# Order and queues of the first loads in a two-layer attention and gated-MLP kernel

## The chip, the cores and the metric

The kernel runs on one core of one Trainium2 chip. The metric is device time in microseconds (us). Before the change it was 1616.12 us, the median of three executions (1615.79 to 1616.38). The whole argument is about the first 23 us of those 1616. "Fast" is the state of an execution with an undisturbed clock.

An execution has a *span*, from its first instruction to its last. The profile shows it, and it is about 1.8 us shorter than the device time.

## The reference, cut to what matters

The input is `x` of 2048 tokens by 1024 features in bf16. Two layers follow, each an attention block (sliding window of 8 keys, stride 2) and a gated MLP, with a layernorm in front of each block. The opening does only this:

```python
xn  = layernorm(x)              # 2048 x 1024
q   = xn @ wqkv[:, 0:1024]      # the query third comes first
```

For the first 512 tokens (one chunk) the kernel computes `q` from four *tiles* of 128 tokens (`x_sb[0]` to `x_sb[3]`, 256 KB each) and eight *rows* of the weight (128 x 1024, 256 KB each). Row k is what the features 128k to 128k+127 are multiplied by. These are 3 MB of first loads.

## The kernel before

The kernel builds a list of operations with estimated durations. `place()` simulates them and fixes each engine's order. Each engine executes in that order, and waits are by semaphore.

```python
def dma(kb, dst, src, reads, writes, cls=3, transpose=False, queue="SP"):
    def emit(op):
        if queue == "AQ":
            nc.scalar.dma_start(dst, src)       # ScalarE's queue
        elif transpose:
            nc.sync.dma_start_transpose(dst, src)
        else:
            nc.sync.dma_start(dst, src)         # SyncE's queue
    return pr.add(queue, 0.45, emit, reads, writes, cls, size=kb * 1024)

def q_first():
    for hh in range(2):                          # tile 0 in two halves, one on each queue
        dma(128, x_sb[0][:, hh * 512:(hh + 1) * 512], ..., queue="AQ" if hh else "SP")
    dma(256, x_sb[1][:], xin[:, 1, :], ..., queue="AQ")       # tile 1
    rows = q_weights(0, "k", load=False)
    for kk in range(4):
        rows[2](kk)                              # weight rows 0 to 3, SyncE
    load_x(0, 2, 4)                              # tiles 2 and 3, SyncE
    rows[2](4)
    rows[2](5)
    # VectorE sums half of tile 0, ScalarE the other half ...
    rows[2](6, 2, queue="AQ", after=[("part", 1)])   # rows 6 and 7 as one load, ScalarE
    # mean of tile 1 on ScalarE; tiles 0 and 1 are centred, transposed on TensorE, copied out ...
    # ... [cut] ...
    # partial products of tiles 0 and 1: rows 0-2 for tile 0, then for tile 1, then rows 3-7 for both
    for kk, j0, j1 in [(k, j, j + 1) for j in range(2) for k in range(3)] + [(k, 0, 2) for k in range(3, KT)]:
        ...  # 8 matmuls of 128x128 or 128x256, waiting for row kk
    # then "the second query half": tiles 2 and 3 against all eight rows, 64 matmuls of 128x256
```

TensorE's order in the opening is fixed: tile 0's transposes; rows 0 and 1 for tile 0 (16 matmuls); tile 1's transposes; row 2 for tile 0, rows 0 to 2 for tile 1, then row by row for both; transposes of tiles 2 and 3 in front of row 7; row 7; the second half.

The loads draw on eight DMA semaphores. The first eight loads are issued at once, each later one waits at issue until the load that last used its semaphore has landed.

## Time and profile before

| what | us | view |
|---|---|---|
| span of the profiled execution | 1614.2 | page |
| PE (TensorE matmul) busy | 1601.5, 99% | page |
| PE idle before the matmuls of row 4 | 0.91 | timeline |
| row 4 issued, landed | 5.71, 11.11 | chain of waits, single DMA records |

The page's busy time of the engines, and its chain of work that ended last, by engine and by line:

```profile
PE 1601.5 (99%) x7463; PEld 762.6 (47%) x7610; DVE 1121.5 (69%) x1904; ACT 331.3 (21%) x527; POOL 5.2 (0%) x28
...
PE 99%; DMA 1%; issue 0%; SPq 0%; DVE 0%
PE bank L347 98%; DMA slot<-in_A_wqkv_dram 1%; PE bank L523 0%; PE bank L509 0%; PE bank L428 0%; SPq L261 0%; DVE x L688 0%
```

TensorE is the limit, and the only other share that shows at all is 1% of the chain spent waiting for weights. One caution: 7463 matmuls are recorded against 7610 weight loads. 147 matmul records are missing, and each leaves a hole that looks like idle time.

TensorE's timeline in the opening of the kernel before (start and duration in us, line, operation, count; in brackets the idle time in front and what ended it):

```profile
4.98 0.66 PE L428 MATMUL bank<-ident,xn 128*128 128x128 bf16 x8
5.89 1.05 PE L509 MATMUL bank<-hT,slot 128*128 128x128 bf16 x16 [0.25 <-DVE hT L433]
6.96 0.62 PE L428 MATMUL bank<-ident,xn 128*128 128x128 bf16 x8
7.42 2.83 PE L509 MATMUL bank<-hT,slot 128*128 128x128 bf16 x40
11.16 2.79 PE L509 MATMUL bank<-hT,slot 128*128 128x256 bf16 x24 [0.91 <-DMA slot<-in_A_wqkv_dram]
13.79 1.06 PE L428 MATMUL bank<-ident,xn 128*128 128x128 bf16 x16
14.68 1.04 PE L509 MATMUL bank<-hT,slot 128*128 128x256 bf16 x8
15.56 7.15 PE L523 MATMUL bank<-xnT,slot 128*128 128x256 bf16 x64
```

L428 are transposes, L509 the partial products, L523 the second query half, which ends at 15.56 + 7.15 = 22.71. The 0.91 us at 11.16 is the wait for row 4. How it came about is in the chain in order of time, same kernel (start, duration, what):

```profile
1.66 4.03 DMA slot<-in_A_wqkv_dram
5.70 0.02 issue
5.71 5.40 DMA slot<-in_A_wqkv_dram
```

Row 1 was issued at 1.66 and landed 4.03 later. That freed its semaphore, so SyncE could issue row 4 at 5.71, and row 4 took 5.40 us, because tiles 2 and 3 and rows 6-7 were in front of it. The DMA queues of the kernel before, from 5 to 7 us (q1 is SyncE's, q10 ScalarE's; packets, MB, share of the 16 engines' time):

```profile
q1 hardware_dynamic: 403, 0.74, 101.3%
q10 hardware_dynamic: 2, 0.00, 0.5%
```

The same view of the same kernel from 7 to 9 us:

```profile
q10 hardware_dynamic: 266, 0.51, 67.1%
q1 hardware_dynamic: 148, 0.27, 36.1%
```

Rows 6-7, issued on ScalarE at 3.57, moved almost nothing from 5 to 7 us (0.5%) and had two thirds of the engines after that.

### The profile page before, as it was taken

What the parts mean: (1) busy time and instruction counts of PE and PEld (TensorE: products, weight loads), DVE (VectorE), ACT (ScalarE), POOL (GpSimd) and SP (SyncE); (2) the same over time, 40 slices, a digit from 0 to 9 for tenths busy, and PEclk for the clock granted to TensorE, in tenths of its full rate; (3) what the DMA queues carried; (4) which work ended last, traced back from release to release, by engine and by line L of the source; (5) the groups of instructions that cost most, each with busy time, mean ns of one, the idle gap of its engine ahead of it and who ended that gap; (6) DMA issues with size and microseconds to landing.
All of it is one profiled execution on the core that took longest, in us unless ns stands there. A gap on an engine that the chain in (4) does not pass through costs nothing.

```text
span 1614.2 us, 19079 instructions
## 1 busy us (share of the span) xinstructions
PE 1601.5 (99%) x7463; PEld 762.6 (47%) x7610; DVE 1121.5 (69%) x1904; ACT 331.3 (21%) x527; POOL 5.2 (0%) x28
## 2 busy tenths in 40 slices
PE   9999999999999999999999999999999999999999
PEld 6555544444444444444444444444444444444444
DVE  5898888889889888888898729884288832211211
ACT  5423322021211222113211032110321101101110
POOL 1000000000000000000000000000000000000000
PEclk9999999999999999999999999999999999999999
DMA  9834755395548664758645487365873464454451
GB/s 320 228 100 150 224 170 171 118 225 168 171 136 251 195 190 132 217 167 234 189 136 160 160 243 231 122 173 176 253 221 119 158 181 156 144 176 150 156 165 44
DMA packets 350777, 285.80 MB, mean 177 GB/s; under 512 B 72288, under 2 KB 344928, under 8 KB 350688
## 3 DMA queue, kind: packets, MB, share of 16 engines
q1 hardware_dynamic: 350128, 283.67, 58.2%
q8 instruction: 59, 0.97, 0.2%
q10 hardware_dynamic: 560, 0.92, 0.2%
q14 instruction: 30, 0.25, 0.0%
HBM read 238.94 MB, written 29.36 MB: 166 GB/s over the span
## 4 chain that ended last, share of the span: by engine, by line
PE 99%; DMA 1%; issue 0%; SPq 0%; DVE 0%
PE bank L347 98%; DMA slot<-in_A_wqkv_dram 1%; PE bank L523 0%; PE bank L509 0%; PE bank L428 0%; SPq L261 0%; DVE x L688 0%
## 5 line engine op out<-in xcount | busy, mean ns | idle before, releaser
L347 PE MATMUL bank<-xnT,slot 128*128 128x512 bf16 x4955 | 1088.9, 379 | 5.3
L347 PEld LDWEIGHTS <-slot 128*128 128x128 bf16 x5056 | 518.1, 102 | 573.0
L347 PE MATMUL bank<-slot,hT 128*128 128x512 bf16 (+2 forms) x1812 | 387.3, 372 | 1.9
L658 DVE TENSOR_TENSOR hT<-sg,bank 128x512 bf16<-128x512 bf16 x224 | 153.4, 685 | 213.0 <-PE bank L347 196.3
L265 DVE TENSOR_TENSOR scr<-scr 128x1024 bf16<-128x1024 bf16 (+3 forms) x576 | 292.1, 535 | 2.1
L347 PEld LDWEIGHTS <-hT 128*128 128x128 bf16 x1848 | 178.5, 98 | 208.7
L656 ACT ACTIVATE sg<-bank 128x512 bf16<-128x512 f32 x224 | 133.8, 597 | 653.8 <-PE bank L347 613.6
L265 DVE TENSOR_TENSOR scr<-qT,kT 128x2048 bf16<-128x2048 bf16 x128 | 153.7, 1216 | 71.7 <-DMA kT<-qkv_d 70.1
L405 ACT CAST sgt<-bank 128x512 bf16<-128x512 f32 x184 | 107.9, 586 | 290.9 <-PE bank L347 273.1
L265 DVE TENSOR_TENSOR scr<-pA,vT 128x2048 bf16<-128x2048 bf16 x128 | 152.5, 1216 | 0.4
L688 DVE TENSOR_TENSOR x<-x,bank 128x512 bf16<-128x512 bf16 (+1 forms) x66 | 43.7, 669 | 122.7 <-PE bank L347 122.4
L347 PE MATMUL bank<-wo,oT 128*128 128x512 bf16 x502 | 112.6, 379 | 0.5
L313 DVE BATCH_NORM_STATS2 st<-x 128x6 f32<-128x512 bf16 x124 | 81.5, 679 | 11.5 <-DMA x<-in_A_x_dram 11.0
L347 PEld LDWEIGHTS <-oT 128*128 128x128 bf16 x512 | 50.1, 98 | 60.3
L633 DVE TENSOR_TENSOR x<-x,bank 128x512 bf16<-128x512 bf16 x64 | 43.9, 685 | 36.5 <-PE bank L347 35.0
L320 ACT ACTIVATE sd<-mv,epst 128x4 f32<-128x4 f32 (+1 forms) x17 | 5.1, 299 | 182.4 <-DVE mv L316 181.9
L616 DVE STREAM_TRANSPOSE pA<-pB 128x2048 bf16<-128x2048 bf16 x16 | 37.0, 2310 | 0.4
L593 DVE STREAM_TRANSPOSE pB<-pA 128x2048 bf16<-128x2048 bf16 x16 | 37.0, 2310 | 0.4
L656 ACT ACT_TABLE_LOAD x20 | 25.7, 1283 | 51.3 <-PE bank L347 51.1
L265 DVE TENSOR_TENSOR pA<-scr 128x256 bf16<-128x256 bf16 x128 | 35.3, 282 | 0.3
L327 DVE TENSOR_SCALAR xn<-x,mv,rstd 128x1024 bf16<-128x1024 bf16 x62 | 30.8, 541 | 4.6 <-DMA xnT<-xn 4.5
L265 DVE TENSOR_TENSOR oT<-scr 128x256 bf16<-128x256 bf16 x128 | 33.6, 282 | 0.1
(60 smaller groups left out, 210.0 us busy)
## 6 DMA issues: line engine op xcount, KB each, us to landing
slot<-in_B_w_dram SPq DMA_DIRECT2D x160, 1024.0 KB, 5.8
slot<-in_A_wqkv_dram SPq DMA_DIRECT2D x28, 1024.0 KB, 5.2
qkv_d<-sgt SPq DMA_DIRECT2D x92, 256.0 KB, 3.4
qT<-qkv_d SPq DMA_DIRECT2D x16, 512.0 KB, 5.0
slot<-in_B_w_dram SPq DMA_DIRECT2D x16, 512.0 KB, 5.5
kT<-qkv_d SPq DMA_DIRECT2D x14, 544.0 KB, 6.6
vT<-qkv_d SPq DMA_DIRECT2D x14, 544.0 KB, 5.7
out_dram<-x SPq DMA_DIRECT2D x31, 128.0 KB, 4.2
```

Source lines behind the costliest of these rows:

```text
L265: return lambda _: nc.vector.tensor_tensor(o, a, b, op=op)
L313: dve(0.67, lambda _, hh=hh: nc.vector.bn_stats(st[q][:, j, hh, :], x_sb[n][:, hh * 512:(hh + 1) * 512]), [("x", n, hh)] + list(after), [( ...
L320: act(0.3, lambda _: nc.scalar.activation(sd[q][:, j0:j1], mv[q][:, j0:j1, 1], ACTF.Sqrt, bias=epst[:]), [("mv", q, j) for j in range(j0, ...
L327: dve(0.5, lambda _: nc.vector.tensor_scalar(xn[j][:], x_sb[n][:], mv[q][:, j, 0:1], rstd[q][:, j:j + 1], op0=ALU.subtract, op1=ALU.mult), ...
L347: nc.tensor.matmul(bank[a.bank][:, 0:ncol], lhsT=w, rhs=r, start=first and i == 0, stop=last and i == n - 1)
L405: evac(act, 0.59, lambda _, a=a, i=i, m=m: nc.scalar.copy(sgt[i][:, m % 2, :], bank[a.bank][:]), op, [], [("sgt", i, m % 2)], a)
L593: dve(2.31, lambda _: nc.vector.transpose(psmT[:].rearrange("p c d -> p (c d)"), psm[:].rearrange("p w s -> p (w s)")), allA, ["pB"])
L616: dve(2.31, lambda _: nc.vector.transpose(At[:].rearrange("p w s -> p (w s)"), AeT[:].rearrange("p c d -> p (c d)")), ["pB"], allA)
L633: evac(dve, t1(512), lambda _, xs=xs, a=a: nc.vector.tensor_tensor(xs, xs, bank[a.bank][:], op=ALU.add), op, [("x", n, hh)], [("x", n, hh) ...
L656: evac(act, 0.6, lambda _, i=i, a=ag: nc.scalar.activation(sg[i][:], bank[a.bank][:], ACTF.Silu), og, [], [("sg", i)], ag, table="silu")
L658: evac(dve, t1(512), lambda _, i=i, a=au, f=f: nc.vector.tensor_tensor(hT[:, f, :], sg[i][:], bank[a.bank][:], op=ALU.mult), ou, [("sg", i ...
L688: evac(dve, t1(cn), lambda _, xs=xs, a=a, cn=cn: nc.vector.tensor_tensor(xs, xs, bank[a.bank][:, 0:cn], op=ALU.add), op, [("x", n, hh)], [ ...
```

## The change

Its intent: the first loads come in the order in which TensorE needs them, on two queues. ScalarE's holds three at once (half of tile 0, tile 1, row 2), then tile 2. SyncE's has the rest.

```diff
         dma(256, x_sb[1][:], xin[:, 1, :], [], [("x", 1, 0), ("x", 1, 1)], 0, queue="AQ")
         rows = q_weights(0, "k", load=False)
         wslots[0] = rows[:2]
-        for kk in range(4):
+        for kk in (0, 1, 3, 4):
             rows[2](kk)
-        load_x(0, 2, 4)
-        rows[2](4)
+        rows[2](2, queue="AQ")
+        load_x(0, 3, 4)
         rows[2](5)
+        rows[2](6, 2)
... [cut]
-        rows[2](6, 2, queue="AQ", after=[("part", 1)])
+        dma(256, x_sb[2][:], xin[:, 2, :], [("part", 1)], [("x", 2, 0), ("x", 2, 1)], 0, queue="AQ")
... [cut]
         for j in range(2, TPC):
-            stats(j)
+            stats(j, [("ce", 1, 0)])
```

In the compiled instruction streams TensorE, VectorE and GpSimd keep exactly the same order. ScalarE swaps two tiny square roots, and the loads move.

## The prediction

> **What bounds the kernel now.** TensorE: the page gives PE busy 1601.5 of 1614.2 us, and the chain of waits is 99% PE, 98% of it the big matmul line. In the timeline only three PE idle times exceed 0.06 us, all in the opening: 0.15 before the first transposes (4.98), 0.25 before the first projection matmul (5.89), 0.91 (10.25 to 11.16) before the partial products of weight rows 4 and later. The rest are 0.05 us pieces, one per 49 matmuls, and a fixed tail. So the change can win little over 0.91.
>
> **Why the 0.91 is there.** Row 4 landed at 11.11. It was issued only at 5.71: eight DMA semaphores are used in turn, so the ninth and later loads wait, at issue, for the load eight before (tile 3 for row 0, landed 4.96; row 4 for row 1, landed 5.70). Tile 2 (issued 3.08), rows 6-7 (ScalarE, 3.57) and tile 3 went ahead, though needed later. From 5 to 15 us the DMA moves 383 to 392 GB/s (256 KB each 0.67 us): order is the limit. The Trainium skill, "DMA: Bandwidth & Descriptors", section "Issuing engines are not separate DMA queues", says that loads of both issuers share 16 engines and interleave; the trace agrees on the shared rate. Yet rows 6-7, issued at 3.57, got almost no packets from 5 to 7 us (0.5% of engine time against 101%) and 67% in 7 to 9: service roughly follows issue order.
>
> **What the change does.** No instruction added or removed; PE, DVE and POOL orders are identical, ScalarE swaps two tiny roots. The first eight loads (no wait) become halves of tile 0, rows 0, 1, 3, 4, tile 1, row 2. Then tile 3 waits for tile 0's first half (3.3), tile 2 on ScalarE for row 0 (about 5.0), row 5 for row 1, rows 6-7 after it. Estimates from 0.67 us per 256 KB: rows 1 and 2 share and land near 6.4 (row 1 was 5.70, row 2 6.53), row 3 at 7.2, row 4 at 7.9, tile 3 at 8.6, tile 2 at about 9, row 5 at 9.9, rows 6-7 at 11.2. PE wants row 4 at 10.25, row 5 at 11.2, row 6 at 12.1: the 0.91 goes. Transposes of tiles 2 and 3 would be wanted at 13.1; they should be ready at 12.7 and 13.3, just in time.
>
> **Cost.** ScalarE now issues tile 2 at 5.0 to 5.4 (one issue takes 0.39 us), in front of its mean of tile 1, which started at 5.24. That mean, and so tile 1's transposes (6.96), moves by about 0.2 us. PE has 0.02 us of slack there, so some 0.2 comes back as a new wait at 7 us.
>
> **Sum.** -0.91 + 0.2 = -0.7 us, all on the critical path. Predicted 1615.4 us, range 1614.8 to 1616.1. Chances: faster by over 2% 0.005, within 0.99, slower 0.005.
>
> **What would show it.** Timeline: no PE idle near 10.3; row 4 landing near 8; second query half ending 0.7 us earlier (22.7 before); mean of tile 1 at 5.4 to 5.5; PE idle of 0.1 to 0.3 near 7.
>
> **What would make it wrong.** Tiles 2 and 3 land after 9.5 and the wait moves to the transposes near 13 us (gain 0.3 or less); row 1 lands past 6.6; ScalarE's issue costs nothing (gain 0.9); K weights or DMA transposes, wanted at 22.0, come late; chips differ by more than the effect.

## The result, and the profile after

The median is 1615.36 us (six executions, 1615.13 to 1616.30) against 1616.09 for the kernel before (six, 1615.79 to 1616.38), so 0.73 us less. The ratio is 0.9997, with an interval of 0.9984 to 1.001. (A ratio is the mean time of one kernel's fast runs over that of the other's of the same rounds, so not quite the ratio of the medians quoted.) The mean gained less than the median, because one of the six took 1616.30. The profile fell on just that one.

TensorE's timeline in the opening of the changed kernel, that execution:

```profile
5.02 1.00 PE L428 MATMUL bank<-ident,xn 128*128 128x128 bf16 x8
6.15 0.61 PE L510 MATMUL bank<-hT,slot 128*128 128x128 bf16 x8
7.03 0.62 PE L510 MATMUL bank<-hT,slot 128*128 128x128 bf16 x8 [0.27 <-DMA slot<-in_A_wqkv_dram]
7.57 0.62 PE L428 MATMUL bank<-ident,xn 128*128 128x128 bf16 x8
8.03 4.58 PE L510 MATMUL bank<-hT,slot 128*128 128x128 bf16 x56
13.40 1.05 PE L510 MATMUL bank<-hT,slot 128*128 128x256 bf16 x8 [0.79 <-DMA slot<-in_A_wqkv_dram]
14.28 1.06 PE L428 MATMUL bank<-ident,xn 128*128 128x128 bf16 x16
15.18 1.04 PE L510 MATMUL bank<-hT,slot 128*128 128x256 bf16 x8
16.05 7.15 PE L524 MATMUL bank<-xnT,slot 128*128 128x256 bf16 x64
```

(Lines have moved by one: L510 and L524 are L509 and L523 of before.) The wait for row 4 is gone: 56 matmuls run through from 8.03. Two waits are new, 0.27 us in front of row 1's matmuls and 0.79 us in front of row 6's. The second half ends at 23.20, later than the 22.71 of before. The chain in order of time, changed kernel:

```profile
1.66 5.32 DMA slot<-in_A_wqkv_dram
6.98 0.02 issue
7.00 0.33 SPq L261
7.32 0.04 issue
7.37 5.98 DMA slot<-in_A_wqkv_dram
```

Row 1, issued at 1.66 as before, took 5.32 us instead of 4.03. Rows 6-7, issued at 7.37, took 5.98 us and landed at 13.35. The DMA queues of the changed kernel, from 5 to 7 us:

```profile
q1 hardware_dynamic: 287, 0.52, 71.1%
q10 hardware_dynamic: 138, 0.25, 33.7%
```

Row 2, issued on ScalarE at 1.69 (0.03 us after row 1 on SyncE), does take a third of the engines while row 1 is wanted. From 5 to 6 us alone it is half: 50.5% for ScalarE's queue, 52.3% for SyncE's. Sums from 9 to 12 us in the changed kernel (busy of PE, PEld, DVE, ACT, POOL, then clock, DMA share, GB/s):

```profile
9.00:12.00 3.00, 3.00 (x38) 2.77 (x36) 2.31 (x5) 2.31 (x6) 0.00 (x0) 1.00 0.88 288
```

Before, this stretch had a DMA share of 1.05 and 395 GB/s. Fewer bytes moved here, while rows 5 to 7 were on their way.

The times at which the loads landed, each read from its single DMA record in the traces (us; the last four columns are experiments):

| load | before | after | after_again | after_third | order_one_queue | tile2_act_only |
|---|---|---|---|---|---|---|
| row 0 | 4.96 | 5.38 | 5.01 | 4.81 | 4.94 | 4.90 |
| tile 1 | 5.15 | 5.57 | 5.21 | 5.01 | 5.18 | 5.19 |
| row 1 | 5.70 | 6.98 | 7.03 | 7.40 | 5.83 | 5.85 |
| row 2 | 6.53 | 7.30 | 7.23 | 8.15 | 6.81 | 6.68 |
| row 4 | 11.11 | 8.34 | 8.39 | 9.01 | 8.39 | 8.51 |
| tile 2 | 8.65 | 9.66 | 9.72 | 10.35 | 9.07 | 8.74 |
| tile 3 | 10.44 | 9.01 | 9.16 | 9.74 | 9.76 | 9.41 |
| row 5 | 11.79 | 10.65 | 10.34 | 10.99 | 10.39 | 10.06 |
| rows 6-7 | 9.74 | 13.35 | 12.21 | 12.36 | 11.75 | 11.43 |

### The profile page after: what moved, and what is told of

It is laid out like the page before. It is cut to its first block, busy times and chain, and to the rows that moved or that the text cites. A ratio compares the mean times of both kernels' runs of the same rounds, so it can differ in the third digit from the quotient of the medians.

```text
span 1614.5 us, 19227 instructions
## 1 busy us (share of the span) xinstructions
PE 1609.9 (100%) x7610; PEld 763.0 (47%) x7610; DVE 1121.6 (69%) x1904; ACT 330.8 (20%) x527; POOL 5.3 (0%) x28
## 4 chain that ended last, share of the span: by engine, by line
PE 99%; DMA 1%; SPq 0%; issue 0%; DVE 0%
PE bank L347 98%; DMA slot<-in_A_wqkv_dram 1%; PE bank L524 0%; PE bank L510 0%; SPq L261 0%; PE bank L428 0%; DVE x L689 0%
## 5 line engine op out<-in xcount | busy, mean ns | idle before, releaser
L313 DVE BATCH_NORM_STATS2 st<-x 128x6 f32<-128x512 bf16 x124 | 81.5, 680 | 12.2 <-DMA x<-in_A_x_dram 11.8
```

The source lines that it names most:

```text
L313: dve(0.67, lambda _, hh=hh: nc.vector.bn_stats(st[q][:, j, hh, :], x_sb[n][:, hh * 512:(hh + 1) * 512]), [("x", n, hh)] + list(after), [( ...
```

## The experiments

**How they were built.** A first attempt only edited the load lines. In the build, `place()` then settled on a different order for the rest of the program, from about TensorE's 1720th instruction on, which would have mixed two effects. So each experiment takes the order that `place()` finds for the changed kernel, and emits only the twelve opening loads anew, from a list of (load, queue). With the changed kernel's own list this gives its instruction streams exactly. In all of them TensorE, VectorE and GpSimd keep the changed kernel's streams.

```python
placed = pr.place()
rest = [o for o in placed if o not in loads.values()]
for name, queue, behind in plan:          # behind: None, or the ScalarE result it follows
    loads[name].eng = queue
    ...
for op in rest[:at] + front + rest[at:]:
    op.emit(op)
```

Below, `S:` is SyncE's list and `A:` ScalarE's; x0a and x0b are the halves of tile 0, x1 to x3 the tiles, r0 to r67 the rows. The changed kernel is `S: x0a r0 r1 r3 r4 x3 r5 r67`, `A: x0b x1 r2 | x2`, where `|` stands for ScalarE's sum of tile 0. All experiments give correct results. Each was run five times, beside nine executions of the kernel before on the same chip. There were three chips, and the kernel before had medians of 1615.94, 1615.88 and 1615.98 on them, so medians from different chips can be compared to about 0.1 us. Where intervals are not quoted they all reach over 1.0 (of the ratio). What counts is whether the executions overlap, and what the traces show.

**One reading serves for all.** In all thirteen traces, the span less the end of the second query half is 1591.31 to 1591.33 or 1591.50 to 1591.51 us. The opening decides all but 0.2 us of a difference between these executions. Two limits of the traces: each run has one, of one of its executions, and the idle time in brackets is printed only from 0.15 us on and leaves out what the modelled ends of the matmuls hide. Where it matters, start times are compared instead.

| kernel | early on ScalarE | median us | lowest to highest | second half ends (trace) |
|---|---|---|---|---|
| before | x0b x1 | 1616.09 (6) | 1615.79 to 1616.38 | 22.71 |
| before_again | x0b x1 | 1615.89 | 1615.76 to 1616.14 | 22.59 |
| after | x0b x1 r2 | 1615.36 (6) | 1615.13 to 1616.30 | 23.20 |
| after_again | x0b x1 r2 | 1615.43 | 1615.03 to 1616.54 | 22.33 |
| after_third | x0b x1 r2 | 1615.63 | 1615.04 to 1616.58 | 22.96 |
| tile2_on_sync | x0b x1 r2 | 1615.76 | 1615.04 to 1617.47 | 24.18 |
| row4_on_act | x0b x1 r4 | 1615.16 | 1614.93 to 1616.88 | 21.85 |
| two_rows_on_act | x0b x1 r2 (r4) | 1616.20 | 1615.39 to 1617.08 | 23.97 |
| order_one_queue | x0b x1 | 1614.98 | 1614.84 to 1615.30 | 21.72 |
| order_one_queue_again | x0b x1 | 1614.94 | 1614.73 to 1615.12 | 21.80 |
| tile2_act_only | x0b x1 | 1614.97 | 1614.83 to 1615.45 | 21.68 |
| mean_delayed | x0b x1 | 1615.07 | 1614.79 to 1615.70 | 22.55 |
| row4_first | x0b x1 | 1616.24 | 1616.02 to 1616.44 | 23.13 |

### after_again

The same instructions as the changed kernel. Edit: none.

> The changed kernel once more (the same instructions on every engine), to see whether its one trace is typical: in it the second query half ended at 23.2 us, later than before (22.7), although most of its executions were faster. Theory (the order of loads closes the wait for row 4, a late mean of tile 1 costs 0.2): median 1615.2 to 1615.6, and in the new trace no idle near 10 us, none over 0.3 near 12.6, the second query half ending at 21.9 to 22.2. Rival A (the wait only moves to rows 6 and 7, and the faster times are chance): the new trace again has idle of 0.5 to 0.9 us before row 6, ends at 22.7 or later, and the median is within 0.2 of before.

The median is 1615.43, as expected. TensorE's timeline in the opening of after_again:

```profile
6.13 0.61 PE L510 MATMUL bank<-hT,slot 128*128 128x128 bf16 x8
7.08 0.62 PE L510 MATMUL bank<-hT,slot 128*128 128x128 bf16 x8 [0.33 <-DMA slot<-in_A_wqkv_dram]
7.53 0.61 PE L428 MATMUL bank<-ident,xn 128*128 128x128 bf16 x8
7.98 5.45 PE L510 MATMUL bank<-hT,slot 128*128 128x128 bf16 x64
...
15.18 7.15 PE L524 MATMUL bank<-xnT,slot 128*128 128x256 bf16 x64
```

No wait for row 4 and none for row 6. The second half ends at 22.33, not quite the 21.9 to 22.2 expected, because the wait at 7 us is 0.33. So the 0.79 us of the first trace does not belong to every execution, but the wait for row 1 was there again. The highest of the five was 1616.54: slow executions did recur.

### before_again

The kernel before against itself.

> The kernel before against itself, a control for noise. Every theory: ratio 1.0000, median 1615.9 to 1616.3, and in its trace again idle of 0.8 to 1.0 us before the matmuls of row 4. If its median strays by 0.3 us from the other runs of before, differences of 0.7 us cannot be read from five rounds.

The median is 1615.89, against 1615.94 of the nine beside it, so five executions of this kernel settle a few tenths of a us. (The 1615.9 expected as the lower bound was missed by 0.01.) The wait for row 4 was 0.45 us this time, below the expected 0.8 to 1.0: tile 0's second half landed at 4.01 instead of 3.54, TensorE began its products 0.5 us later, and part of the wait for row 4 was hidden. How much a removed wait is worth therefore varies with the execution; the end of the half (22.59 against 22.71) hardly moved.

### tile2_on_sync

```diff
-S: x0a r0 r1 r3 r4 x3 r5 r67      A: x0b x1 r2 | x2
+S: x0a r0 r1 r3 r4 x2 x3 r5 r67   A: x0b x1 r2
```

> The change without its ScalarE issue of tile 2: SyncE issues tile 2 after row 4 and before tile 3; every compute instruction stays where it is. Theory (that issue delays the mean of tile 1 by 0.2 us): the mean of tile 1 starts within 0.1 us of the landing of tile 1, PE idle near 7 us falls by about 0.2, and the median is 0.1 to 0.3 us below that of after_again. Rival B (the issue on ScalarE costs nothing; tile 1 lands late because three loads share the start): the mean starts as late as in after_again and the median is the same within 0.1.

The mean of tile 1 did start 0.09 us after tile 1 landed (5.19), against 0.27 in after_again, so the delay by ScalarE's issue is real: 0.18 us. But nothing was won: the median went up to 1615.76. TensorE's timeline of tile2_on_sync:

```profile
7.50 0.62 PE L510 MATMUL bank<-hT,slot 128*128 128x128 bf16 x8 [1.10 <-DMA slot<-in_A_wqkv_dram]
7.95 0.61 PE L428 MATMUL bank<-ident,xn 128*128 128x128 bf16 x8
8.40 4.58 PE L510 MATMUL bank<-hT,slot 128*128 128x128 bf16 x56
14.38 1.05 PE L510 MATMUL bank<-hT,slot 128*128 128x256 bf16 x8 [1.41 <-DMA slot<-in_A_wqkv_dram]
```

This was the slowest execution of the five (1617.47). Row 1 landed at 7.45 and rows 6-7 at 14.34. The mean of tile 1 was on time and TensorE waited for row 1 all the same. So the mean was not what TensorE waited for here. Whether a late mean would cost anything if row 1 were in time, this run cannot say. A new theory for the wait takes over (theory D in what follows): a load issued early on ScalarE shares the engines with the load that SyncE issues at the same time.

### order_one_queue

```diff
-S: x0a r0 r1 r3 r4 x3 r5 r67         A: x0b x1 r2 | x2
+S: x0a r0 r1 r2 r3 r4 x2 x3 r5 r67   A: x0b x1
```

> Order of need alone: as tile2_on_sync, but row 2 goes back to SyncE too, so ScalarE's queue holds only half of tile 0 and tile 1, as before. Theory (order is what pays, the second queue adds no bandwidth): row 1 lands 0.3 to 0.7 us earlier than in after_again because row 2 no longer shares with it, the wait for row 4 stays closed, median 1615.0 to 1615.5. Rival C (the gain comes from issuing on two queues): row 4 lands as late as before, near 11 us, and the median is back at 1616.0.

Row 1 landed at 5.83, 1.20 us earlier than in after_again and more than expected, row 4 at 8.39, and the median is 1614.98. TensorE's timeline of order_one_queue:

```profile
5.27 0.66 PE L428 MATMUL bank<-ident,xn 128*128 128x128 bf16 x8 [0.17 <-DVE xn L464]
6.18 1.05 PE L510 MATMUL bank<-hT,slot 128*128 128x128 bf16 x16 [0.25 <-DVE hT L433]
7.07 0.61 PE L428 MATMUL bank<-ident,xn 128*128 128x128 bf16 x8
7.52 5.45 PE L510 MATMUL bank<-hT,slot 128*128 128x128 bf16 x64
...
14.57 7.15 PE L524 MATMUL bank<-xnT,slot 128*128 128x256 bf16 x64
```

From 6.18 on there is no wait at all. Its sums from 9 to 12 us, to be held against 288 GB/s in the changed kernel:

```profile
9.00:12.00 3.00, 3.00 (x34) 2.73 (x32) 2.84 (x8) 2.13 (x7) 0.00 (x0) 1.00 1.05 404
```

So the order of need is worth about 1 us, and the second queue takes part of it away again. Rival C, that two queues are what pays, falls.

### tile2_act_only

```diff
-S: x0a r0 r1 r3 r4 x3 r5 r67      A: x0b x1 r2 | x2
+S: x0a r0 r1 r2 r3 r4 x3 r5 r67   A: x0b x1 | x2
```

> The other corner of the square: row 2 is back on SyncE, tile 2 stays on ScalarE behind its sum of tile 0. With one load fewer early on ScalarE the semaphore it reuses is that of tile 0's first half, not of row 0, so it should be issued at 3.4 to 4.0 us instead of 5.0. Theory D (early sharing of row 1 with row 2 is what costs; a load issued later on ScalarE waits its turn behind what was issued before): row 1 lands at 5.7 to 6.2, the mean of tile 1 starts within 0.15 us of its landing, no idle above 0.1 near 7 us, median 1614.8 to 1615.2 with a spread under 0.6. Rival E (any load on ScalarE's queue behind tile 1 slows and scatters the transfers): median 1615.3 to 1615.8, spread over 1 us, fewer than 170 KB per half microsecond between 9 and 12 us.

Row 1 landed at 5.85, the mean started at 5.28, and the median is 1614.97 with a spread of 0.62 (under 0.6 was expected). Tile 2 was issued on ScalarE at 3.54, and that queue had 0.5% of the engines from 5 to 7 us: it waited its turn. With tile2_on_sync and order_one_queue this closes the square: with row 2 early on ScalarE 1615.43 and 1615.76, without it 1614.97 and 1614.98, and where tile 2 is issued makes no difference that shows beside that. It does not isolate the cost of tile 2's wait for row 0, since here it reuses another semaphore and is issued long before the mean. Rival E falls: it is not the use of ScalarE's queue as such.

### row4_on_act

```diff
-S: x0a r0 r1 r3 r4 x3 r5 r67      A: x0b x1 r2 | x2
+S: x0a r0 r1 r2 r3 x2 x3 r5 r67   A: x0b x1 r4
```

> Row 4 instead of row 2 takes the third early place on ScalarE; row 2 is on SyncE behind row 1; tile 2 is on SyncE. Theory D (whatever is issued third on ScalarE at 1.7 us shares the engines with row 1): row 1 lands at 6.8 to 7.5 as in after_again, row 2 at 7.3 to 8, idle of 0.3 to 1 us before the matmuls of row 1 or 2, median 1615.3 to 1616.0. Rival F (only rows 1 and 2 side by side are slow, for instance neighbouring addresses): row 1 lands before 6.3 and the median is 1614.8 to 1615.2.

This lies between the two theories. Row 1 landed at 6.39, row 2 at 7.40, without a wait in front of their matmuls, and the median is 1615.16. Theory D's ranges for row 1 and the median are missed; rival F's median fits, its row 1 does not. But that trace is of the third fastest of five, and two of the five took 1616.38 and 1616.88. No execution without a third early load on ScalarE was that slow, apart from those of row4_first and of the kernel before. Row 4 took 31% of the engines from 5 to 7 us, so it does share; row 1 lost less by it than when row 2 stood there. Rows 1 and 2 side by side may be worse than other pairs; one trace does not settle it.

### two_rows_on_act

```diff
-S: x0a r0 r1 r3 r4 x3 r5 r67   A: x0b x1 r2 | x2
+S: x0a r0 r1 r3 x2 x3 r5 r67   A: x0b x1 r2 r4
```

> The suspected cost doubled: rows 2 and 4 both go early on ScalarE's queue, rows 1 and 3 on SyncE's, tiles 2 and 3 on SyncE. Theory (early loads on the second queue share with SyncE's and leave late rows and slow executions): row 1 at 6.8 to 7.5, row 3 at 8.0 or later (7.4 to 7.8 with one queue), median 1615.3 to 1616.2, spread over 1 us. Rival H (one shared pair is enough to unsettle it, a second adds nothing): as after_third within 0.2. Rival C (two evenly loaded queues are good): median under 1615.0.

The suspected cost doubled makes it worse: median 1616.20, spread 1.69, row 1 at 7.53, row 3 at 8.19. Rival H expected the time of after_third (1615.63) and falls. Row 4 is here the ninth load, so it waited for a semaphore and was issued at 3.25, not quite as early as intended.

### row4_first

The smallest edit of the kernel before, to see whether row 4 alone was the obstacle:

```diff
-S: x0a r0 r1 r2 r3 x2 x3 r4 r5   A: x0b x1 | r67      (the kernel before)
+S: x0a r0 r1 r2 r3 r4 x2 x3 r5   A: x0b x1 | r67
```

> The smallest edit of the kernel before: row 4 moves in front of tiles 2 and 3, rows 6 and 7 stay on ScalarE behind its sum of tile 0. Theory: idle before row 4 vanishes, but row 5, still behind rows 6 and 7 and tiles 2 and 3, lands near 11.7 and is wanted at 11.3, so idle of 0.3 to 0.7 us stands before row 5 and the median is 1615.4 to 1615.8. Rival: row 4 alone was the obstacle, no idle is left and the median is 1614.8 to 1615.2 as with order_one_queue.

TensorE's timeline of row4_first:

```profile
7.46 3.70 PE L510 MATMUL bank<-hT,slot 128*128 128x128 bf16 x48
11.89 1.92 PE L510 MATMUL bank<-hT,slot 128*128 128x256 bf16 x16 [0.73 <-DMA slot<-in_A_wqkv_dram]
14.00 1.27 PE L428 MATMUL bank<-ident,xn 128*128 128x128 bf16 x16 [0.19 <-DVE xn L327]
```

The wait moved one row on, to row 5 (landed 11.85), 0.73 us long. Then tile 3, landed at 11.18 instead of 10.44, made its transposes late too, and the chain of work that ended last runs through tile 3. The median of 1616.24 misses the expected 1615.4 to 1615.8 and is 0.36 above the nine executions of before beside it (1615.88). The rival falls: one load moved forward pushes others back, and the gain only comes when the whole list is in order of need.

### mean_delayed

order_one_queue with one more ScalarE instruction, to test the prediction's second term alone:

```diff
+ scalar.activation(xn[3][:, 0:16], x_sb[1][:, 0:16], Copy)    # between tile 1's landing and its mean
```

> order_one_queue with one tiny extra ScalarE copy of 128x16 (its result is overwritten) between tile 1's landing and its mean, to delay that mean by 0.2 to 0.3 us without touching any load. The prediction's step (0.02 us of slack there, so a delayed mean is paid in full): idle of 0.2 to 0.3 us before tile 1's transposes near 7 us, median 0.15 to 0.35 above order_one_queue (1614.98). Rival: there is slack elsewhere and the median moves by less than 0.1.

The median is 1615.07, 0.09 above order_one_queue (on another chip) and 0.10 above tile2_act_only on the same chip. That is less than the 0.15 to 0.35 of the prediction's step, and 0.1 is at the edge of what five executions can tell. The trace, though, shows the step at work. It is of the slowest execution (1615.70), in which tile 1 itself landed at 5.83, 0.65 us later than in order_one_queue. The mean began 0.34 us after that instead of 0.09, and TensorE then waited 0.88 us for VectorE's centred tile 1 and for nothing else that shows:

```profile
7.89 0.62 PE L428 MATMUL bank<-ident,xn 128*128 128x128 bf16 x8 [0.88 <-DVE xn L464]
```

So there the 0.25 us of delay was paid. In order_one_queue, order_one_queue_again and tile2_act_only tile 1 was centred only 0.13, 0.09 and 0.08 us before its transposes began, so there is little slack. Whether such a delay is usually paid stays open: the medians say hardly, this trace says yes.

### order_one_queue_again and after_third

The candidate and the changed kernel once more, together on another chip.

> order_one_queue once more on this chip, as the candidate that beats both kernels. Theory: median 1614.8 to 1615.2, spread under 0.8, no idle over 0.1 behind the first projection matmul. If chance chose it the first time, the median is within 0.2 of after_third.

The median is 1614.94, the spread 0.39, and the idle column of the trace shows no wait behind the first projection matmul. Start times show one: from the 64 partial products (7.29) to the next transposes (12.78) it took 5.49 us, against 5.28 in order_one_queue, because row 6 landed only at 11.85. So the expectation of no idle over 0.1 was missed by 0.1.

> The changed kernel a third time, for its spread beside order_one_queue_again on one chip. Theory (a third early load on ScalarE leaves some executions with late rows): median 1615.2 to 1615.6, at least one of five over 1616.0, row 1 landing at 6.8 to 7.5 in the trace. Rival: the spread seen so far was chance, all five within 0.6.

The median is 1615.63 (0.03 above the range expected), and two of five were over 1616.0. In the trace row 1 landed at 7.40 and TensorE waited 0.70 us for it. Tile 2, landed at 10.35, made the transposes of tiles 2 and 3 late as well: they began 5.48 us after the 64 partial products (8.35 to 13.83), against 5.28 in order_one_queue, and row 7 followed 1.11 us later (14.94), against 0.90. TensorE's timeline of after_third:

```profile
8.35 5.45 PE L510 MATMUL bank<-hT,slot 128*128 128x128 bf16 x64
13.83 1.27 PE L428 MATMUL bank<-ident,xn 128*128 128x128 bf16 x16
14.94 1.04 PE L510 MATMUL bank<-hT,slot 128*128 128x256 bf16 x8
```

So order_one_queue beats both kernels by its median: its ten executions on two chips lie between 1614.73 and 1615.30, the eighteen executions of the kernel before beside them between 1615.56 and 1616.19, and the two do not overlap. The changed kernel's executions do overlap with its own (they begin at 1615.03), but on each chip its median is higher, by 0.45 and 0.69 us. Against the kernel before it is 1.0 us of median, and its interval (0.998 to 1.0007) allows for no change.

## Why the prediction was right, and where only its sum was

**Total.** 1615.4 was predicted and 1615.36 measured. The three series of the changed kernel gave 1615.36, 1615.43 and 1615.63.

**"-0.91": the wait for row 4 goes.** Right. No trace of the changed kernel has idle time near 10.3, and row 4 landed at 8.3 to 9.0 (about 7.9 predicted). order_one_queue shows that order of need does it, without the second queue; row4_first shows that row 4's place alone does not.

**"Rows 1 and 2 share and land near 6.4."** This is the step that was mis-sized. They landed at 6.98 to 7.40 and 7.23 to 8.15. The estimate let each load cost 0.67 us and started from row 1 alone. Here is what it left out. A load counts as landed when the last of its 16 parts has, and the kept traces hold the time of each part (the updates of the load's semaphore, which no view above prints). In after_again 15 parts of row 1 were in at 6.03 and the last at 7.03; in the first trace 15 at 6.39 and the last at 6.98; in after_third they came in one by one from 5.27 to 7.40. So 6.4 was about right for most of the row, and the late parts cost the rest. Between the first and the last part of row 1 lay 1.5 to 2.3 us in the five traces with row 2 early on ScalarE, 0.66 in row4_on_act, and 0.3 to 0.7 with only two loads early there, but for mean_delayed (1.17). Why a part is late, no run here shows.

**"+0.2": ScalarE's issue delays the mean of tile 1, and TensorE pays.** The delay was right: 0.26 to 0.28 us from tile 1's landing to its mean in the three traces of the changed kernel, against 0.09 before. Whether TensorE pays for it is not settled. In these three traces another wait lies over it: TensorE waited for row 1, by 0.27, 0.33 and 0.70 us. VectorE had tile 1 centred at 7.51, 7.14 and 6.94, and its transposes began at 7.57, 7.53 and 7.90, so only in the first trace did they follow it at once. A similar delay alone (mean_delayed) moved the median by 0.1, and was paid in the one trace. The 0.02 us of slack was read from one trace; the first projection matmul started at 5.89 there and at 6.42 in before_again, and the slack in front of tile 1 moves with it. So idle near 7 us was foretold in the right place and size, but what ended it was row 1. That two sizes fitted was luck.

**"Tiles 2 and 3 just in time."** Tile 3 at 9.0 to 9.7 and tile 2 at 9.7 to 10.4 were later than predicted (8.6 and about 9). In the first trace the later row 6 hides this, and in after_again it cost about 0.1 us. In after_third the transposes were late by 0.4 us in all, which is the failure that the prediction had named for tiles landing after 9.5.

**"Rows 6-7 at 11.2."** They landed at 12.2 to 13.4, and in the first trace TensorE waited 0.79 us for them: 13 of their 16 parts were in at 11.98, and the last three came from 13.25 to 13.35. The prediction named no such wait.

**What the prediction did not see: spread.** With a third load early on ScalarE, 8 of 31 executions (four kernels) took over 1616.2 us. With two, in order of need, none of 20 did, and the slowest took 1615.70. In the five traces with row 2 early on ScalarE the DMA moved 288 to 352 GB/s from 9 to 12 us; in the seven traces with only two loads early there, 371 to 404. So early sharing and a lower rate long after the shared loads have landed go together in these five traces (three of them are of the slowest execution of their run, but so are two of the seven). That one causes the other is not shown: the packet records don't tell the 16 engines apart, and row4_on_act, with a third early load, kept 387 GB/s in its one, fast, trace.

## What to carry to other kernels

When an opening waits for loads, write down when each is needed and issue them all in that order: here, moving one forward only moved the wait to the next. The second queue gave no more bandwidth here (381 GB/s from 5 to 9 us before, 386 after), so put on it only what is needed at the same moment as its neighbour on the first queue, or what is issued late enough to queue behind. Judge a gain of less than 0.1% by many executions and several traces: here one trace of the better kernel showed a worse opening than one of the kernel before.

## What the Trainium skill lacked or had wrong

- The Trainium skill's page "DMA: Bandwidth & Descriptors", section "Issuing engines are not separate DMA queues", says that issuing from several engines only saves the sequencer's time. The shared rate agrees (381 to 386 GB/s from 5 to 9 us before and after). It has no figure for what the interleaving does to the load that is waited for: row 1 came at 7.0 to 7.5 with row 2 beside it on ScalarE (five traces), and at 5.6 to 6.3 with only two loads early there (seven).
- The same page, section "Queues, rings and completion order", says that each engine takes turns, packet by packet, between the queues that have work for it. This fits a load issued at 1.69 us (50.5% of the engines for ScalarE's queue from 5 to 6 us, 52.3% for SyncE's). It does not show for those issued at 3.54 and 3.57, which had 0.5% from 5 to 7 us and moved in the order of issue. Whether their descriptors had reached the engines by then, no record tells.
- No page that I found says how far apart the 16 parts of one load land: for row 1, 1.5 to 2.3 us in the five traces with row 2 early on the second queue, 0.3 to 1.2 in the seven with only two loads early there.
- No page that I found has the fall of rate after early sharing: 288 to 352 GB/s from 9 to 12 us in the five traces with row 2 early on the second queue, 371 to 404 in the seven with only two loads early there.
- No page that I found has what the ninth load waits for: row 4, issued at 5.71, had waited for the landing of row 1 at 5.70, because eight DMA semaphores are used in turn.
